# A fused attention and routed-layer kernel: the queue order and buffers of the weight pieces in its first stage

## The chip, the cores and the metric

The kernel runs on one core of one Trainium2 chip. The metric is the device time of one execution in microseconds (us). TensorE (PE) multiplies matrices, VectorE (DVE), ScalarE (ACT) and GpSimd (POOL) work element by element, and SyncE (SP) issues most transfers (DMA) between the device memory and the memory on the chip. Every engine has its own stream of instructions and works it off in order; semaphores tie the streams together.

## The reference, cut to what matters

```python
scale = 1.0 / np.sqrt(64)
p_packed = sm_attn(p, k, v)              # 32 packed queries per head over 576 keys; 8 batches, 8 heads
attn = sm_attn(q, p_packed, p_packed)    # 576 queries over the 32 packed rows
x = attn.transpose(0, 2, 1, 3).reshape(4608, 512)
h = x @ w_in                             # w_in 512 x 2048
x = (h - np.tanh(h)) @ w_out             # w_out 2048 x 512
logits = x @ w_gate                      # then: one of 8 experts for each token,
out = gate * eom * (relu(x @ w1[e]) @ w2[e])
```

q, k, v and p arrive as 32-bit floats. The weights w_in and w_out arrive as 64-bit floats, and the kernel narrows them to 32 bits itself, in pieces of 128 rows by 512 columns.

## The kernel before, in words

The program has three parts. **The first stage** computes the packed attention of p over k and v. It is cut into 16 units (`UNITS`), each for four heads of a batch, and its loop runs `u` from 0 to 17, so that the parts of one unit overlap those of its neighbours. In pass `u`, TensorE does the scores of unit `u` (`score`), the transposes of k for unit `u + 1` (`k_up`, three groups), and the product with v for unit `u - 2` (`pack`). VectorE takes the maximum (`expo`) and the transpose of the exponentials (`e_up`); ScalarE copies the transposed k, takes the exponential (`expo_b`) and scales the result of `pack`. The tiles are `kt` and `vt` (k and v as loaded), `kT`, `sc` (scores), `e_sb`, `eT`, `po` and `pp`. Beside that run `jobs`: the second attention of the first half batch, in steps `att_q`, `make_z`, `att_s`, `att_f`, `att_x`, `att_n`, `att_t`, `att_l`, and the product `fuse` of the packed rows with w_in.

In the same stage the weights are narrowed. `plan` lists 32 pieces, first 16 of w_in and then 16 of w_out. A piece is loaded into a staging tile `st` of 4 KB a partition (`load_w_in`, `load_w_out`), ScalarE takes the absolute value of its high words (L105), GpSimd bounds it from below (L106), and VectorE puts the words together in three steps (L111, L112, L114). Of a w_out piece, ScalarE and VectorE then make a high and a low part (`part_out`, L150 and L151). `NA` pieces are converted in the first stage, spread over the passes; `load_ahead(done)` issues loads until `NST` pieces more than those done are under way, and `NST` staging buffers turn in a circle.

**The second stage** works on halves of batches. Each half has 16 steps `f`: `up` (six matmuls), `up_b`, `down` (twelve matmuls), with 288 columns each; `drain` follows. Its first half also converts the pieces that the first stage left over, in steps 0 onwards, and does the second attention of the next half in steps 4 to 11. **The third part** routes tokens to experts. It isn't touched by the change.

What sets the order of work is the text of the program: each engine gets its instructions in the order in which the functions are called. All loads of k, v, p, q and the weights stand in SP's one queue, in that order, and a load whose buffer is still in use holds up all loads behind it.

```python
            want = (NA * u + LA - 2) // (LA - 1)
            for x, (_, conv, n) in enumerate(plan[done:want]):
                convert(done + x)
                if conv is conv_out:
                    late.append(n)
            done = want
            load_ahead(done)
            if u < 2:
                load_q(0, 0, [2 * u, 2 * u + 1])
```

Of the kernel before, what the change touches and what calls it, by code (L numbers as in the profile page):

```python
# [37 lines left out]
NST = 3  # L38
UNITS = 2 * NB
NA = 20  # L40
# [3 lines left out]
def attention_moe_kernel(ctx: ExitStack, tc: tile.TileContext, q, k, v, p, w_in, w_out, w_gate, w_og, w1, w2, out):  # L44
# [85 lines left out]
    wst, ist = {}, {}  # L130

    def load_w_out(f):
        rows = w_out[128 * f:128 * f + 128]
        if w_out.dtype == F32:
            wst[f] = cv.tile([128, DM], F32, name="wf")
            sp.dma_start(wst[f], rows)
        else:
            wst[f] = cv.tile([128, DM, 2], I32, name="st", bufs=NST)
            sp.dma_start(wst[f].rearrange("p n w -> p (n w)"), rows.bitcast(I32))
# [13 lines left out]
    def load_w_in(n):  # L153
        m, j = divmod(n, 4)
        rows, cols = slice(128 * j, 128 * j + 128), slice(512 * m, 512 * m + 512)
        if w_in.dtype == F32:
            sp.dma_start(w_in_sb[:, j, cols], w_in[rows, cols])
        else:
            ist[n] = cv.tile([128, 512, 2], I32, name="st", bufs=NST)
            sp.dma_start(ist[n].rearrange("p n w -> p (n w)"), w_in[rows, cols].bitcast(I32))  # L160
# [151 lines left out]
    def load_ahead(done):  # L312
        while ahead[0] < min(len(plan), done + NST):
            fn, _, n = plan[ahead[0]]
            fn(n)
            ahead[0] += 1
# [4 lines left out]
    with ExitStack() as pa:  # L321
# [3 lines left out]
        kp = pa.enter_context(tc.tile_pool(name="kp", bufs=3))  # L325
# [49 lines left out]
        load_ahead(1 - NST)  # L375
        load_k(1)
        load_ahead(2 - NST)
# [3 lines left out]
        load_ahead(0)  # L381
# [45 lines left out]
        for a in range(4):  # L427
            r = slice(32 * a, 32 * a + 32)
            pool.tensor_copy(fold[r], ident[r, r].rearrange("p (o c) -> p o c", o=1).to_broadcast([32, 4, 32]))
        jobs = {3: [lambda: att_q(0, 0)], 4: [lambda: make_z(0), lambda: att_s(0, 0)], 5: [lambda: att_f(0, 0), lambda: att_x(0, 0)],  # L430
                6: [lambda: att_n(0, 0), lambda: att_t(0, 0), lambda: fuse(0, 0)], 7: [lambda: att_l(0, 0), lambda: fuse_h(0, 0), lambda: fuse_l(0, 0)]}
        late, done = [], 0
        LA = UNITS + 2
        for u in range(LA):
# [8 lines left out]
            if u + 1 < UNITS:  # L443
                k_up(u + 1, 2)
            if 1 < u < UNITS + 2:
                pack(u - 2)
            if u + 1 < UNITS and (u + 1) % 4 == 0:
                make_p((u + 1) // 4)
            if u < UNITS:
                expo_b(u)  # L450
            for fn in jobs.get(u, ()):
                fn()
            if u + 3 < UNITS:
                load_k(u + 3)
            if 0 < u < UNITS:
                load_v(u)
            if u in (1, 5):
                load_p(2 + u // 4)
            if u % 4 == 2 and u < UNITS - 4:
                dup_p(u // 4 + 1)  # L460
            if u == 4:
                load_gates()
            if u == 7:
                vec.tensor_copy(wgt[:, :, 0:2 * NE], wgr)
# [9 lines left out]
            load_ahead(done)  # L474
            if u < 2:
                load_q(0, 0, [2 * u, 2 * u + 1])
# [4 lines left out]
    with ExitStack() as pb:  # L481
# [193 lines left out]
        for i, (b, hf) in enumerate(halves):  # L675
# [12 lines left out]
            if i == 0:  # L688
# [6 lines left out]
                for f in range(NF):  # L695
                    for x in part:
                        at(0, f, part_out, x)
                    part = []
                    take = plan[done:done + (2 if len(plan) - done > NF - 3 - f else 1)]
                    for x, (_, conv, m) in enumerate(take):  # L700
                        at(0, f, convert, done + x)
                        if conv is conv_out:
                            part.append(m)
                            assert f + 1 < m
                        else:
                            assert f < (0, 0, 4, 8)[m // 4]
                    done += len(take)
                    at(0, f, load_ahead, done)
# [469 lines left out]
```

## Time and profile before

| what | value |
|---|---|
| median of 3 runs | 1346.26 us (1340.08 to 1346.48) |
| the profiled execution, its own time | 1350.53 us |
| its span, first to last instruction | 1348.6 us |
| mean granted TensorE clock | 0.975 of full speed |
| busy: PE, DVE, ACT, POOL | 1264.3, 811.3, 515.1, 319.1 us |

The profile is that of one execution. Its times count from the span's start. A row of the timeline gives start, length, engine, source line, operation and operands, and in square brackets how long the engine stood idle before it and what ended the wait; "issue" there means that nothing which the profile shows was waited for. The granted clock is 1.00 at 2.4 GHz and 0.50 at 1.2 GHz. Loads of k and v are 576 KB each, those of weight pieces 512 KB. Engines that are not the bottleneck may idle at no cost, so the busy times are to be read by stage: the second stage begins at 122.71 us, with the first `up` matmul on TensorE.

### The profile page before, as it was taken

The page shows a single profiled execution, that of the slowest core. Times are in us where ns is not written, and L with a number is a line of the kernel's source. Part 1 is how long each engine was busy: PE and PEld are TensorE (multiplying, and loading weights), DVE is VectorE, ACT ScalarE, POOL GpSimd, SP SyncE. Part 2 cuts the span into 40 slices and gives each one's busy share as a digit, 9 for nine tenths or more (in the row PEclk, how much of TensorE's full clock was granted, in tenths as well). Part 3 has the DMA queues.
Part 4 walks back from the last instruction along what each step waited for, and adds up shares of the span by engine and source line. Part 5 has one row for each costly group of instructions (what it writes and reads, how often), then busy time and mean ns, then how long its engine had stood idle before and what let it go on. Part 6 is the DMA issues. An engine that isn't in the chain of part 4 may idle for free. (4 is left out here: it accounts for less than half of the span.)

```text
span 1348.6 us, 28576 instructions
## 1 busy us (share of the span) xinstructions
PE 1264.3 (94%) x10464; PEld 1084.6 (80%) x10464; DVE 811.3 (60%) x1823; ACT 515.1 (38%) x1109; POOL 319.1 (24%) x383
## 2 busy tenths in 40 slices
PE   6768779999999999999999999979999999999987
PEld 4556668998988989989899799757888788778765
DVE  4757887777777767777767867552333433433651
ACT  4344444344344343443434445332223322422431
POOL 4323311001010010100100111124443544354531
PEclk8789889999999999999999999989999999999999
DMA  8874524014122140142203134521113311412331
GB/s 254 292 255 150 143 49 25 13 36 36 32 25 17 36 36 7 35 32 36 30 8 54 19 50 116 130 76 40 48 39 106 108 48 39 161 50 94 125 143 42
DMA packets 135757, 102.42 MB, mean 76 GB/s; under 512 B 96784, under 2 KB 115220, under 8 KB 134964
## 3 DMA queue, kind: packets, MB, share of 16 engines
q1 hardware_dynamic: 125908, 80.33, 25.4%
q0 software_dynamic: 9696, 20.14, 5.1%
q8 instruction: 85, 1.39, 0.5%
q14 instruction: 68, 0.56, 0.2%
HBM read 215.60 MB, written 19.57 MB: 174 GB/s over the span
## 5 line engine op out<-in xcount | busy, mean ns | idle before, releaser
L616 POOL DMA_INDIRECT tab<-tok,ix x48 | 55.0, 1146 | 614.0 <-DVE ix L613 566.0
L883 DVE TENSOR_TENSOR hl<-pt,hh 128x512 fp32r<-128x512 f32 x76 | 52.3, 689 | 191.2 <-ACT hh L882 180.6
L522 ACT ACTIVATE gh<-gg 128x288 fp32r<-128x288 f32 x256 | 112.7, 440 | 142.0 <-PE acc L537 95.7
L523 DVE TENSOR_TENSOR gl<-gg,gh 128x288 fp32r<-128x288 f32 x256 | 115.4, 451 | 81.6 <-ACT gh L522 76.1
L509 PE MATMUL ph<-a_hi,wf_hi 128*128 128x288 f32 x512 | 160.1, 313 | 3.0 <-ACT wf_hi L240 3.0
L536 PE MATMUL acc<-gl,wo_bt 128*128 128x288 f32 x512 | 155.4, 304 | 4.4 <-DVE gl L523 4.0
L511 PE MATMUL ph<-a_hi,wf_lo 128*128 128x288 f32 x512 | 152.0, 297 | 5.5 <-DVE wf_lo L244 5.5
L515 DVE TENSOR_TENSOR gg<-ph,th 128x288 f32<-128x288 f32 x256 | 115.9, 453 | 68.5 <-ACT th L513 66.9
L535 PE MATMUL acc<-gh,wo_a 128*128 128x288 f32 x512 | 151.5, 296 | 2.0 <-ACT gh L522 2.0
L536 PE MATMUL acc<-gl,wo_a 128*128 128x288 f32 x512 | 151.9, 297 | 1.3 <-DVE gl L523 1.3
L535 PE MATMUL acc<-gh,wo_bt 128*128 128x288 f32 x512 | 152.2, 297 | 0.6 <-ACT gh L522 0.6
L510 PE MATMUL ph<-a_lo,wf_hi 128*128 128x288 f32 x512 | 151.8, 297 | 0.8 <-issue 0.8
L537 PE MATMUL acc<-gh,wo_bt 128*128 128x288 f32 x512 | 152.0, 297 | 0.0
L537 PE MATMUL acc<-gh,wo_a 128*128 128x288 f32 x512 | 151.7, 296 | 0.0
L827 POOL DMA_INDIRECT xg<-x2d,iq x132 | 135.1, 1023 | 61.1 <-issue 52.9
L513 ACT ACTIVATE th<-ph 128x288 f32<-128x288 f32 x256 | 104.1, 407 | 113.7 <-PE ph L511 92.8
L871 ACT ACTIVATE h<-ph 128x512 f32<-128x512 f32 x76 | 45.0, 597 | 249.8 <-PE ph L870 199.3
L509 PEld LDWEIGHTS ph<-a_hi,wf_hi 128*128 128x128 f32 x512 | 96.6, 189 | 45.2 <-issue 39.5
L869 PE MATMUL ph<-w1l,xh 128*128 128x512 f32 x304 | 121.3, 399 | 6.8 <-DVEq L1004 5.9
L892 PE MATMUL py<-w2h,hh 128*128 128x512 f32 x304 | 126.1, 415 | 0.2
L893 PE MATMUL py<-w2l,hh 128*128 128x512 f32 x304 | 120.3, 396 | 1.7 <-DVE w2l L788 1.7
L894 PE MATMUL py<-w2h,hl 128*128 128x512 f32 x304 | 120.6, 397 | 0.7 <-DVE hl L883 0.7
(220 smaller groups left out, 2715.4 us busy)
## 6 DMA issues: line engine op xcount, KB each, us to landing
raw<-in_moe_w_dram SPq DMA_DIRECT2D x37, 2048.0 KB
sraw<-in_moe_w_dram SPq DMA_DIRECT2D x37, 1024.0 KB
x2s<-in_moe_w_dram SPq DMA_DIRECT2D x37, 1024.0 KB
kt<-in_k_dram SPq DMA_DIRECT2D x16, 576.0 KB
vt<-in_v_dram SPq DMA_DIRECT2D x16, 576.0 KB
x2d<-x2s SPq DMA_DIRECT2D x64, 144.0 KB
qt<-in_q_dram SPq DMA_DIRECT2D x240, 36.0 KB
st<-in_moe_w_in_dram SPq DMA_DIRECT2D x16, 512.0 KB
```

The source lines that it names most:

```text
L509: pe.matmul(ph, lhsT=wf_hi[n][:, g, c], rhs=ah[:, g], start=g == 0, stop=False)
L510: pe.matmul(ph, lhsT=wf_hi[n][:, g, c], rhs=al[:, g], start=False, stop=False)
L511: pe.matmul(ph, lhsT=wf_lo[n][:, g, c], rhs=ah[:, g], start=False, stop=g == 1)
L515: vec.tensor_tensor(gg, ph, th, op=ALU.subtract)
L535: pe.matmul(acc[j], lhsT=hi[:, j], rhs=gh, start=f == 0, stop=False)
L536: pe.matmul(acc[j], lhsT=hi[:, j], rhs=gl, start=False, stop=False)
L537: pe.matmul(acc[j], lhsT=lo[:, j], rhs=gh, start=False, stop=f == NF - 1)
L827: pool.indirect_dma_start(xg[:, g], None, src, bass.IndirectOffsetOnAxis(ap=iq[:, g:g + 1].bitcast(U32), axis=0))
L869: pe.matmul(ph, lhsT=xh[:, c], rhs=w1l[:, c, r], start=False, stop=False)
L892: pe.matmul(py, lhsT=hh[:, c], rhs=w2h[:, c], start=c == 0, stop=False)
L893: pe.matmul(py, lhsT=hh[:, c], rhs=w2l[:, c], start=False, stop=False)
L894: pe.matmul(py, lhsT=hl[:, c], rhs=w2h[:, c], start=False, stop=c == 7)
```

## The change

The change does six things. It raises `NA` from 20 to 24. It gives the staging tiles of the first 24 pieces two buffers more (`NX`, a pool `cx`, so five in all) and k four buffers instead of three. It moves `load_ahead` from the end of a pass, behind that pass's conversions, to a place ahead of them and behind the loads of k and v, with the count of pieces done up to the pass before. It loads q one part in each of passes 2 to 5, instead of two parts in each of passes 0 and 1, and moves `jobs` from passes 3 to 7 to passes 6 to 10. It loads k of unit 3 and v of unit 1 before the loop. And it puts the exponential `expo_b` ahead of `pack` and `make_p` in a pass. In the second stage `load_ahead` moves ahead of the step's conversion in the same way.

```diff
+NX = 2
-NA = 20
+NA = 24
...
+    extra = {}
+
+    def stage(i):
+        pl = extra["pool"] if i < NA and i % (NST + NX) >= NST else cv
+        return pl.tile([128, 512, 2], I32, name="st", bufs=NX if pl is not cv else NST)
+
-            wst[f] = cv.tile([128, DM, 2], I32, name="st", bufs=NST)
+            wst[f] = stage(i)
...
-            ist[n] = cv.tile([128, 512, 2], I32, name="st", bufs=NST)
+            ist[n] = stage(i)
...
     def load_ahead(done):
-        while ahead[0] < min(len(plan), done + NST):
+        while ahead[0] < len(plan) and ahead[0] < done + NST + (NX if ahead[0] < NA else 0):
             fn, _, n = plan[ahead[0]]
-            fn(n)
+            fn(n, ahead[0])
             ahead[0] += 1
...
-        kp = pa.enter_context(tc.tile_pool(name="kp", bufs=3))
+        kp = pa.enter_context(tc.tile_pool(name="kp", bufs=4))
+        extra["pool"] = pa.enter_context(tc.tile_pool(name="cx", bufs=1))
...
         load_k(0)
         load_p(0)
-        load_ahead(1 - NST)
+        load_ahead(1 - NST - NX)
         load_k(1)
-        load_ahead(2 - NST)
+        load_ahead(2 - NST - NX)
         load_v(0)
         load_k(2)
         load_p(1)
-        load_ahead(0)
+        load_ahead(3 - NST - NX)
+        load_k(3)
+        load_v(1)
...
-        jobs = {3: [lambda: att_q(0, 0)], 4: [lambda: make_z(0), lambda: att_s(0, 0)], 5: [lambda: att_f(0, 0), lambda: att_x(0, 0)],
-                6: [lambda: att_n(0, 0), lambda: att_t(0, 0), lambda: fuse(0, 0)], 7: [lambda: att_l(0, 0), lambda: fuse_h(0, 0), lambda: fuse_l(0, 0)]}
+        jobs = {6: [lambda: att_q(0, 0)], 7: [lambda: make_z(0), lambda: att_s(0, 0)], 8: [lambda: att_f(0, 0), lambda: att_x(0, 0)],
+                9: [lambda: att_n(0, 0), lambda: att_t(0, 0), lambda: fuse(0, 0)], 10: [lambda: att_l(0, 0), lambda: fuse_h(0, 0), lambda: fuse_l(0, 0)]}
...
+            if u < UNITS:
+                expo_b(u)
             if 1 < u < UNITS + 2:
                 pack(u - 2)
             if u + 1 < UNITS and (u + 1) % 4 == 0:
                 make_p((u + 1) // 4)
-            if u < UNITS:
-                expo_b(u)
-            for fn in jobs.get(u, ()):
-                fn()
-            if u + 3 < UNITS:
+            if 0 < u and u + 3 < UNITS:
                 load_k(u + 3)
-            if 0 < u < UNITS:
+            if 1 < u < UNITS:
                 load_v(u)
+            load_ahead(done)
             if u in (1, 5):
                 load_p(2 + u // 4)
+            if 1 < u < 6:
+                load_q(0, 0, [u - 2])
...
+            for fn in jobs.get(u, ()):
+                fn()
...
             done = want
-            load_ahead(done)
-            if u < 2:
-                load_q(0, 0, [2 * u, 2 * u + 1])
...
+                    if f:
+                        at(0, f, load_ahead, done)
                     take = plan[done:done + (2 if len(plan) - done > NF - 3 - f else 1)]
...
-                    at(0, f, load_ahead, done)
```

SP's queue, from its ninth load on, before (`kt`, `vt` are k and v, `st` a weight piece, `scr` of q or p):

```order
L160 DMA st<-in_moe_w_in_dram 128x1024
L257 DMA kt<-in_k_dram 128x1152
L187 DMA scr<-in_q_dram 32x9x32 x8
L257 DMA kt<-in_k_dram 128x1152
L262 DMA vt<-in_v_dram 128x1152
L371 DMA scr<-in_p_dram 128x4x64
L160 DMA st<-in_moe_w_in_dram 128x1024 x2
L187 DMA scr<-in_q_dram 32x9x32 x8
L257 DMA kt<-in_k_dram 128x1152
L262 DMA vt<-in_v_dram 128x1152
```

And with the change, from the same load on:

```order
L166 DMA st<-in_moe_w_in_dram 128x1024
L263 DMA kt<-in_k_dram 128x1152
L268 DMA vt<-in_v_dram 128x1152
L166 DMA st<-in_moe_w_in_dram 128x1024 x2
L263 DMA kt<-in_k_dram 128x1152
L378 DMA scr<-in_p_dram 128x4x64
L263 DMA kt<-in_k_dram 128x1152
L268 DMA vt<-in_v_dram 128x1152
L166 DMA st<-in_moe_w_in_dram 128x1024 x2
L193 DMA scr<-in_q_dram 32x9x32 x4
```

The sixth load of k, the next to last `kt` row in both lists, stood behind sixteen transfers of q and behind two weight pieces that wait for a conversion; it now stands behind weight pieces with free buffers, and ahead of all q.

ScalarE in the first stage, passes 1 to 3 before (`cvt<-st` is the first step of a conversion):

```order
L291 ACTIVATE e_sb,rs<-sc,mx 128x576
L105 ACTIVATE cvt<-st 128x512 x3
L271 ACTIVATE kT<-pk 128x384 x3
L306 ACTIVATE pp<-po,rs 128x64
L291 ACTIVATE e_sb,rs<-sc,mx 128x576
L105 ACTIVATE cvt<-st 128x512
L271 ACTIVATE kT<-pk 128x384 x3
L306 ACTIVATE pp<-po,rs 128x64
L387 ACTIVATE scr<-pk 128x512
L291 ACTIVATE e_sb,rs<-sc,mx 128x576
L105 ACTIVATE cvt<-st 128x512
```

And with the change:

```order
L297 ACTIVATE e_sb,rs<-sc,mx 128x576
L106 ACTIVATE cvt<-st 128x512 x3
L277 ACTIVATE kT<-pk 128x384 x3
L297 ACTIVATE e_sb,rs<-sc,mx 128x576
L312 ACTIVATE pp<-po,rs 128x64
L106 ACTIVATE cvt<-st 128x512
L277 ACTIVATE kT<-pk 128x384 x3
L297 ACTIVATE e_sb,rs<-sc,mx 128x576
L312 ACTIVATE pp<-po,rs 128x64
L396 ACTIVATE scr<-pk 128x512
L106 ACTIVATE cvt<-st 128x512 x2
```

The exponential `e_sb` went ahead of `pp`, which waits for the end of `pack`; and pass 3 has two conversions where it had one.

VectorE in the second stage's first half, from the maximum of step 8 to step 10, with the change (`gl` and `gg` are the step's own work, `cvt` conversions, of which none is left here):

```order
L214 TENSOR_REDUCE amx<-sT 128x18
L215 TENSOR_TENSOR sT<-sT,amx 128x576
L157 TENSOR_TENSOR wo_bt<-cvt,wo_bt 128x512
L532 TENSOR_TENSOR gl<-gg,gh 128x288
L524 TENSOR_TENSOR gg<-ph,th 128x288
L250 TENSOR_TENSOR wf_lo_2340<-px,wf_hi_2339 128x512 x2
L222 TENSOR_REDUCE asm<-ex 128x18
L223 TENSOR_SCALAR asm<-asm 128x18
L224 RECIPROCAL asm<-asm 128x18
L225 TENSOR_TENSOR ex<-ex,asm 128x576
L532 TENSOR_TENSOR gl<-gg,gh 128x288
L524 TENSOR_TENSOR gg<-ph,th 128x288
```

Before, three conversion instructions and one `wo_bt` stood at the end of each of the steps 8 to 11; with the change the last conversion is in step 7 and its `wo_bt` in step 8.

## Rows read from the trace of the kernel before

**Rows 1.** Windows by stretch: length, busy us (instructions) by engine, clock, DMA share, GB/s
```profile
0.00:23.20 23.20, 16.16 (x260) 12.72 (x261) 6.45 (x11) 10.50 (x22) 11.36 (x35) 0.85 0.85 277
77.20:98.20 21.00, 12.43 (x343) 9.17 (x344) 9.44 (x22) 6.78 (x17) 3.69 (x4) 0.80 0.89 325
80.00:85.00 5.00, 3.92 (x42) 2.67 (x45) 2.59 (x7) 1.47 (x3) 1.46 (x2) 0.50 1.01 390
167.90:189.70 21.80, 13.69 (x73) 12.54 (x73) 18.85 (x35) 9.04 (x19) 5.05 (x4) 0.83 0.35 76
199.80:240.00 40.20, 40.20 (x335) 35.53 (x334) 29.10 (x72) 16.91 (x41) 4.19 (x6) 1.00 0.37 26
```

**Rows 2.** Timeline, PE, first stage: start, length, idle before and its releaser
```profile
34.47 2.15 PE L270 MATMUL pk<-ident,kt 128*128 128x128 f32 x9 [3.43 <-DMA kt<-in_k_dram]
...
48.40 1.18 PE L303 MATMUL po<-vt,eT 32*32 32x64 f32 x55 [2.79 <-issue]
...
81.08 1.18 PE L280 MATMUL sc<-kT,scr 64*32 64x288 f32 x5 [3.17 <-issue]
...
95.44 1.22 PE L303 MATMUL po<-vt,eT 32*32 32x64 f32 x73 [3.59 <-issue]
...
104.62 0.96 PE L280 MATMUL sc<-kT,scr 64*32 64x288 f32 x16
105.51 1.20 PE L270 MATMUL pk<-ident,kt 128*128 128x128 f32 x9
...
109.09 0.68 PE L303 MATMUL po<-vt,eT 32*32 32x64 f32 x33 [0.69 <-issue]
109.70 0.72 PE L280 MATMUL sc<-kT,scr 64*32 64x288 f32 x16
...
114.92 0.72 PE L280 MATMUL sc<-kT,scr 64*32 64x288 f32 x16 [0.22 <-ACT kT L271]
...
119.96 0.52 PE L303 MATMUL po<-vt,eT 32*32 32x64 f32 x20 [1.29 <-DMA vt<-in_v_dram]
```

**Rows 3.** DMA queues from 0 to 122.7 us: packets, MB, share of 16 engines
```profile
q1 hardware_dynamic: 14461, 30.47, 72.7%
q8 instruction: 20, 0.33, 1.0%
```

**Rows 4.** Waits, 20 to 123 us: who waited for whom, us, times, longest
```profile
PE po L303 <- issue: 9.0, 6, 3.6
...
PE sc L280 <- issue: 5.8, 2, 3.2
PE pk L270 <- DMA kt<-in_k_dram: 3.4, 1, 3.4
...
PE sc L280 <- ACT e_sb L291: 1.4, 1, 1.4
```

**Rows 5.** Timeline, SP: the loads around k of unit 5
```profile
24.27 5.97 SPq L187 DMA_DIRECT2D scr<-in_q_dram  x8
30.34 0.40 SPq L257 DMA_DIRECT2D kt<-in_k_dram  x1
```

**Rows 6.** Costliest groups, DVE, 0 to 123 us: busy, mean ns
```profile
L112 DVE SCALAR_TENSOR_TENSOR cvt<-st,cvt 128x512 int32<-128x512 int32 x18 | 12.8, 712 | 0.6
L114 DVE SCALAR_TENSOR_TENSOR w_in_sb<-st,cvt 128x512 int32<-128x512 int32 x16 | 11.4, 710 | 0.5
L111 DVE TENSOR_SCALAR cvt<-cvt 128x512 int32<-128x512 int32 x18 | 8.9, 495 | 11.6 <-POOL cvt L106 11.6
L151 DVE TENSOR_TENSOR wo_a<-cvt,wo_a 128x512 fp32r<-128x512 f32 x1 | 0.7, 692 | 1.7 <-ACT wo_a L150 1.7
```

**Rows 7.** Timeline, DVE: a pass with two conversions
```profile
107.97 0.82 DVE L111 TENSOR_SCALAR cvt<-cvt 128x512 int32<-128x512 int32 x1 [4.82 <-POOL cvt L106]
```

**Rows 8.** Timeline, DVE, second stage, first half: steps 8 and 12 begin
```profile
167.95 0.45 DVE L523 TENSOR_TENSOR gl<-gg,gh 128x288 fp32r<-128x288 f32 x1
...
189.72 0.45 DVE L523 TENSOR_TENSOR gl<-gg,gh 128x288 fp32r<-128x288 f32 x1
```

More of the change, by code (lines that the diff above doesn't have):

```diff
@@ L130, in attention_moe_kernel, with load_w_out @@
     wst, ist = {}, {}
-    def load_w_out(f):
+    extra = {}
+    def stage(i):
+        pl = extra["pool"] if i < NA and i % (NST + NX) >= NST else cv
+        return pl.tile([128, 512, 2], I32, name="st", bufs=NX if pl is not cv else NST)
+    def load_w_out(f, i):
         rows = w_out[128 * f:128 * f + 128]
@@ L151, in part_out, with load_w_in @@
         vec.tensor_tensor(lo, sv, hi, op=ALU.subtract)
-    def load_w_in(n):
+    def load_w_in(n, i):
         m, j = divmod(n, 4)
```

## The prediction

> **What bounds the kernel now.** I read the busy time by stretch first. From 199.8 us on TensorE is busy in all 40.20 of 40.20 us [rows 1], and the rest of the second stage looks the same, so whatever the front of the program gains or loses reaches the end one for one. The change acts ahead of that, in two stretches with different limits.
>
> In the first stage (0 to 122.7 us) no engine is full. Between 77.2 and 98.2 us TensorE is busy 12.43 of 21.00 us, VectorE 9.44, ScalarE 6.78; up to 23.2 us it is 16.16 of 23.20, VectorE 6.45 [rows 1]. The transfers are the busiest resource, with a share of 0.89 in the one stretch and 72.7% over the whole stage [rows 1, 3], but they too have pauses. What the reader is to see in TensorE's timeline are the pauses between passes: 3.43 us for k of unit 5, and stops of 2.79 and 3.59 us in the middle of a row of identical `pack` matmuls, put down to "issue" [rows 2]. Nothing in the program can be waited for there. The stage fetches 20 blocks of instructions by DMA [rows 3]; the reading that fits is that TensorE stands until the next block has come, and that a block comes late while the DMA engines are full. The same kind of stop is 0.69 us at 109 us, where they are nearly empty [rows 2]. Such stops sum to 9.0 + 5.8 = 14.8 us [rows 4], and a long one is followed by the lower of the two levels of TensorE's clock: behind the stop of 3.17 us that ended at 81.08 us [rows 2], the granted clock is 0.50, or 1.2 GHz, from 80 to 85 us [rows 1]. That is why it is 0.80 to 0.85 over these stretches.
>
> In the first half of the second stage, VectorE sets the pace in the steps 8 to 11: 18.85 of 21.80 us busy, TensorE 13.69 [rows 1], and these four steps take 189.72 - 167.95 = 21.77 us [rows 8]. A later half takes about 40.2 / 16 = 2.5 us a step with TensorE full [rows 1].
>
> **The change part by part. Four pieces leave the second stage.** A conversion is three VectorE instructions, 0.495 + 0.712 + 0.710 = 1.92 us by their means, and the split of a w_out piece is another 0.692 [rows 6]; 2.6 us each, 10.4 us for four. They sit in steps 8 to 11 of a stretch that VectorE fills, so they are on the path. From the other side: at 2.5 us a step, with the two extras there (the fused weights and the sums of the attention) still costing 1 to 1.5 us each, the four steps would take about 12 us, so 21.8 - 12 = 9.8. I take **-10**. The bounds are -5 (VectorE's 2.95 us idle in the four steps stays, and the chain through ScalarE's exponential takes 2 us of the rest) and -12 (all steps at 2.5 us: 21.8 - 10).
>
> **Four pieces enter the first stage.** By the same rows that is 7.7 us of conversion and, for the three of them split before the end, 2.1 us: between 0, when they fill VectorE's idle time (9.44 of 21.00 us busy), and +9.8, all on the path. They come mostly as passes with two conversions, seven instead of three. There the second one waits for ScalarE and GpSimd: 4.82 us in the pass at 105 to 110 us [rows 7]. Yet TensorE's pass there took 109.70 - 104.62 = 5.08 us, and the next, with one conversion, 5.22 [rows 2], so what reaches TensorE is about 1 us (the product behind it waited for ScalarE's scaling). Four more such passes: **+4**. This is nearer to the lower bound since that pass is the nearest row.
>
> **The queue.** k of unit 5 was issued at 30.34 us, behind eight q transfers that took 5.97 us to issue [rows 5]; in the new order it stands ahead of all q, and its buffer, of four, is free early. The wait of 3.43 us goes: **-3.4**. v for the last product stood behind weight pieces waiting for conversions; its 1.29 us [rows 2] goes: **-1.3**. After the first 20 us these two are TensorE's only waits for k or v [rows 2, 4]. The weights themselves come two pieces earlier, but VectorE did not wait for them in the middle of the stage, so deeper staging gives nothing by itself. The order of the first eight loads is the same, hence also the start.
>
> **The exponential ahead of pack.** One wait of TensorE for it is shown, 1.4 us [rows 4]: **-1.4**. It also releases the scores one `pack` earlier, which I cost at nothing, since two score buffers cover it; if they don't, it is a further gain.
>
> **The later jobs** move the same VectorE work from passes 3 to 7 to passes 6 to 10; cost 0, covered by VectorE's idle time in 77.2 to 98.2 us [rows 1]. If that cover goes, passes 8 and 10, which have both a job and two conversions, last some 2 us longer each. SP's transfers are as many as before, four weight pieces excepted: 4 x 512 KB at the 325 GB/s of a full stretch [rows 1] are 6.5 us of transfers, in a stage where the engines of DMA stand idle for 27% of 122.7 us, or 33 us [rows 3]. A weight load that waits for a conversion still holds up the k and v behind it on SP, but those are now the next pass's, needed two passes later.
>
> **The instruction stops** I leave as they are. They depend on how full the DMA engines are when a block is asked for; the added 6.5 us raise the share from 0.73 to about 0.78 if the stage lasts as long. Bounds: all 14.8 us gone, or twice as many. Here the row shows stops up to 3.59 us [rows 2]. The Trainium skill (Runtime: NRT & Kernel Launch, "Instruction fetch mechanics") says that instructions stream in blocks of 16 KiB while the current one runs, the cost "mostly hidden". By that rule the stops have another cause, one in the queue that the change may clear, and the sum would be about -11 in the first stage; the trace speaks against it, as the stops lie inside one group of matmuls.
>
> **The sum.** First stage: +4 - 3.4 - 1.3 - 1.4 = -2.1, say -2. Second stage: -10. Together -12 on the profiled execution's own time of 1350.5 (span 1348.6 and 1.9 around it): 1338.5. That execution stands 4.3 above the median of the runs shown; from the median 1346.3 the forecast is **1334 us**. Its own range is 1326 to 1341.
>
> **The rivals.** *The stage runs freely.* If transfers that no longer queue behind conversions also end most of the stops and the low clock after them, the first stage goes to what its loops need. From 23.2 us on come thirteen passes at 5.2 us [rows 2], six of them 1 us longer for the second conversion, some 8 us more for what of the jobs VectorE can't hide (an estimate), and 6.5 us for the last products, which is what they take now: 23.2 + 67.6 + 6 + 8 + 6.5 = 111 us, so -11, and with -10 in the second stage -21: 1325 us. For it: passes at 104 to 119 us did run so. Against: they ran so beside nearly empty DMA engines.
>
> *The stops multiply.* With five staging buffers and four of k, SP has a load in the engines almost always, and each of the 20 fetches, TensorE's and the others', can meet one. Eight such stops are in the stage now [rows 4]. A long one costs some 2.7 us more than one beside empty engines, and 1.7 us more by the low clock behind it (half of a stretch at half speed: `k_up` took 2.15 us behind the wait at 34 us and 1.20 at 105 us [rows 2], and a `pack` loses about as much): some 4.4 each. Three more outweigh the gain of 12; five more give +22, so about 1356 us, slower. For it: the stops did come with full engines. Against: the same bytes per pass, and a fetch is passed on a queue of its own, so that the length of SP's queue need not matter.
>
> *The pieces are paid for where they go.* VectorE's path in the first stage carries all 9.8 us, seven double passes in a row with the jobs, while the queue's gain of 6.1 and the 10 of the second stage stand against it, less 3 us that the next piece arrives late in steps 2 and 3, since it now queues behind sixteen transfers of q: -3 to -6, about 1342 us, within the noise.
>
> *It doesn't do what it says*: the extra buffers are used only if SP isn't stopped elsewhere. Then the queue terms go and -10 + 4 = -6 is left, 1340 us; I put that with the case before.
>
> **How the numbers follow.** Chances: forecast 0.46, free stage 0.23, paid for 0.21, stops multiply 0.10. A difference of 0.5% (6.7 us) is about what a measurement of this kernel can tell from none. Faster by more: most of the forecast (0.40), the free stage (0.23), a little of the third case (0.05): 0.68. Slower by more: the stops (0.09): 0.09. The rest, 0.23, is within. The range runs from 1317, the bounds of both stages together with some of the stops gone (-12 and -17), to 1346, no change; what is left out is most of the stops case and the ends of the others.
>
> **What would show it.** Right: the second stage's first `up` at 118 to 123 us; no wait for `kt` after 20 us; SP's weight loads waiting little for VectorE; steps 8 to 11 of the first half in about 12 us. The forecast is wrong if the second stage starts before 115 or after 128 us, or if steps 8 to 11 still take over 16 us. Fewer or more stops put down to "issue", and the clock behind them, tell the first two rivals apart.

## The result, and the profile after

| | before | changed | ratio, 95% interval |
|---|---|---|---|
| median of 5 runs each | 1343.05 us (1340.08 to 1346.48) | 1334.43 us (1333.02 to 1337.38) | 0.9919 [0.9893, 0.9945] |
| the profiled execution, and its span | 1350.53, 1348.6 | 1334.43, 1332.7 | |
| mean granted TensorE clock | 0.975 | 0.982 | |

The ratios and intervals, here and below, are those on record. A ratio is an estimate of its own and not the quotient of the two medians, which is 0.9936 here; the two differ by up to 0.0024 (3 us).

The change makes the kernel faster by 8.6 us at the medians. The profiled executions differ by 15.9 us in span, but not all of that is the change's: behind the first half's drain the span is 1150.1 us before and 1146.4 after, and the other traces of the same two kernels have 1142.0 and 1136.6 there. So the traces are compared up to that drain, which starts at 198.46 us before and at 186.33 us after.

Windows of the kernel after. The columns are those of [rows 1]; the stretches are the same 21 us of the first stage, the end of it (from the scores of the last unit to the first step of the second stage), the steps 8 to 11, and a later half:

```profile
77.20:98.20 21.00, 16.23 (x506) 13.07 (x505) 17.40 (x35) 11.47 (x27) 6.74 (x5) 0.80 0.73 262
109.20:137.68 28.48, 19.36 (x516) 16.42 (x514) 24.77 (x49) 13.92 (x31) 10.60 (x7) 0.88 0.44 129
165.37:177.72 12.35, 9.49 (x57) 8.80 (x57) 9.64 (x20) 5.38 (x12) 0.00 (x0) 0.86 0.00 1
187.90:228.10 40.20, 40.20 (x335) 35.53 (x334) 28.99 (x73) 16.86 (x40) 4.20 (x6) 1.00 0.34 30
```

The third row is the largest gain: steps 8 to 11 take 12.35 us where they took 21.77 [rows 8], and VectorE is busy 9.64 us in them instead of 18.85 [rows 1]. The fourth is the same as before: TensorE is full there. The second is where the four pieces are paid for: VectorE is busy 24.77 of 28.48 us.

TensorE's timeline of the kernel after, first stage; columns as in [rows 2]:

```profile
23.43 1.59 PE L276 MATMUL pk<-ident,kt 128*128 128x128 f32 x9 [2.54 <-DMA kt<-in_k_dram]
...
42.36 0.75 PE L309 MATMUL po<-vt,eT 32*32 32x64 f32 x38 [3.15 <-issue]
...
48.97 2.36 PE L309 MATMUL po<-vt,eT 32*32 32x64 f32 x80 [3.05 <-issue]
...
75.68 1.54 PE L286 MATMUL sc<-kT,scr 64*32 64x288 f32 x16 [2.71 <-ACT e_sb L297]
...
92.33 1.22 PE L286 MATMUL sc<-kT,scr 64*32 64x288 f32 x16 [3.68 <-ACT scr L396]
...
109.20 0.72 PE L286 MATMUL sc<-kT,scr 64*32 64x288 f32 x16
113.19 3.62 PE L309 MATMUL po<-vt,eT 32*32 32x64 f32 x144 [3.27 <-ACT pp L312]
118.90 0.40 PE L518 MATMUL ph<-a_hi,wf_hi 128*128 128x288 f32 x1 [2.09 <-ACT e_sb L297]
```

The wait for k of unit 5 [rows 2] is gone; one of 2.54 us for unit 4 stands eleven us earlier. The stops inside a group are still there. The last scores start at 109.20 us, 5.7 us earlier than before (114.92 [rows 2]), yet the first `up` comes at 118.90, only 3.8 us earlier.

The transfers' queues of the kernel after from 0 to 122 us, columns as in [rows 3]:

```profile
q1 hardware_dynamic: 15040, 32.58, 77.6%
q8 instruction: 20, 0.33, 1.1%
```

The share is 77.6% where it was 72.7% [rows 3]. The waits of the kernel after from 20 to 123 us, as in [rows 4]:

```profile
PE po L309 <- issue: 8.8, 4, 3.1
DVE wo_a L157 <- ACT wo_a L156: 5.9, 3, 4.0
...
PE sc L286 <- ACT scr L396: 4.4, 2, 3.7
...
PE sc L286 <- ACT e_sb L297: 2.7, 1, 2.7
PE pk L276 <- DMA kt<-in_k_dram: 2.5, 1, 2.5
...
PE sc L286 <- issue: 2.3, 2, 1.3
```

New here are the waits of TensorE for ScalarE's copies (4.4 us) and of VectorE for ScalarE's half of a split (5.9 us, the longest 4.0).

VectorE's timeline of the kernel after, the end of the first stage and then three marks of the second: the gated products with which the steps 1, 8 and 12 begin, and the drain:

```profile
117.83 0.77 DVE L301 STREAM_TRANSPOSE eT<-e_sb 128x576 f32<-128x576 f32 x1
...
119.80 0.69 DVE L157 TENSOR_TENSOR wo_a<-cvt,wo_a 128x512 fp32r<-128x512 f32 x1 [0.96 <-ACT wo_a L156]
120.41 0.42 DVE L112 TENSOR_SCALAR cvt<-cvt 128x512 int32<-128x512 int32 x1
...
122.48 0.83 DVE L112 TENSOR_SCALAR cvt<-cvt 128x512 int32<-128x512 int32 x1
...
124.69 0.77 DVE L301 STREAM_TRANSPOSE eT<-e_sb 128x576 f32<-128x576 f32 x1
...
137.68 0.45 DVE L532 TENSOR_TENSOR gl<-gg,gh 128x288 fp32r<-128x288 f32 x1
...
165.37 0.45 DVE L532 TENSOR_TENSOR gl<-gg,gh 128x288 fp32r<-128x288 f32 x1
...
177.72 0.46 DVE L532 TENSOR_TENSOR gl<-gg,gh 128x288 fp32r<-128x288 f32 x1 [0.22 <-ACT gh L531]
...
186.33 1.65 DVE L554 STREAM_TRANSPOSE x2s<-acc 128x288 f32<-128x288 f32 x4
```

Between the last two transposes of the exponentials, on which the last products with v wait, stand a split and two conversions: 6.86 us from the one to the other. Before, it was one conversion and a split, and 5.37 us. The same transposes, the mark of step 1 and the drain in VectorE's timeline of the kernel before:

```profile
118.12 0.77 DVE L295 STREAM_TRANSPOSE eT<-e_sb 128x576 f32<-128x576 f32 x1
...
123.49 0.77 DVE L295 STREAM_TRANSPOSE eT<-e_sb 128x576 f32<-128x576 f32 x1
...
136.05 0.44 DVE L523 TENSOR_TENSOR gl<-gg,gh 128x288 fp32r<-128x288 f32 x1
...
198.46 1.65 DVE L545 STREAM_TRANSPOSE x2s<-acc 128x288 f32<-128x288 f32 x4
```

The mark of step 1 comes at 137.68 us, 1.6 later than before (136.05).

These marks cut the front of the program into five lengths, in us, each the difference of two starts on TensorE's or VectorE's timeline. The table has them for the kernels that follow, but for the last one, one trace each; the ratio is the one on record, to the kernel before on the same chip.

| kernel | to the last scores | end of stage 1 | steps 1-7 | 8-11 | 12 to drain | drain at | ratio |
|---|---|---|---|---|---|---|---|
| before | 114.9 | 21.1 | 31.9 | 21.8 | 8.7 | 198.5 | 1 |
| before, again | 111.7 | 24.4 | 31.4 | 21.8 | 8.8 | 198.0 | 0.9986 |
| changed | 109.2 | 28.5 | 27.7 | 12.4 | 8.6 | 186.3 | 0.9919 |
| changed, again | 113.2 | 30.1 | 28.2 | 12.0 | 8.2 | 191.7 | 0.9901 |
| changed, 20 pieces | 113.8 | 26.3 | 28.4 | 21.8 | 8.8 | 199.0 | 0.9966 |
| changed, three staging buffers | 116.2 | 28.5 | 31.5 | 12.3 | 8.6 | 197.1 | 0.9944 |
| changed, old place of the weight loads | 116.7 | 28.9 | 28.1 | 12.7 | 8.6 | 195.0 | 0.9977 |
| changed, old places of q and jobs | 113.4 | 28.6 | 27.8 | 12.0 | 8.2 | 190.0 | 0.9980 |
| changed, exponential behind `pack` | 112.5 | 30.3 | 28.2 | 12.0 | 8.2 | 191.2 | 0.9907 |
| changed, splits ahead of `pack` | 109.4 | 28.5 | 28.3 | 12.0 | 8.1 | 186.5 | 0.9902 |
| the same, first steps two pieces ahead | 109.5 | 28.9 | 28.3 | 12.0 | 8.2 | 186.9 | 0.9890 |
| before, 24 pieces | 118.2 | 30.3 | 30.9 | 12.1 | 8.2 | 199.6 | 0.9994 |
| before, 24 pieces, five buffers | 115.3 | 30.5 | 31.8 | 12.6 | 8.6 | 198.8 | 1.0024 |

The column of steps 8 to 11 has the pieces in it and repeats to 0.3 us. The end of the stage has them too, 28.5 us or more with 24 pieces and 26.3 or less with 20, but it differs by up to 3.3 us between two traces of one kernel, and the first column by 3 to 4. So a single row's first two columns, and with them its drain, say less than the ratio.

### The profile page after: what moved, and what is told of

It reads as the page before. It is cut to its first block, busy times and chain, and to the rows that moved or that the text cites. A ratio compares the mean times of both kernels' runs of the same rounds, so it can differ in the third digit from the quotient of the medians.

```text
span 1332.7 us, 28571 instructions
## 1 busy us (share of the span) xinstructions
PE 1259.2 (94%) x10464; PEld 1081.7 (81%) x10464; DVE 814.1 (61%) x1823; ACT 516.7 (39%) x1109; POOL 320.6 (24%) x383
## 5 line engine op out<-in xcount | busy, mean ns | idle before, releaser
L524 DVE TENSOR_TENSOR gg<-ph,th 128x288 f32<-128x288 f32 x256 | 116.2, 454 | 68.4 <-ACT th L522 67.0
```

Of the source, the lines that this page charges most:

```text
L524: vec.tensor_tensor(gg, ph, th, op=ALU.subtract)
```

## The experiments

**The kernels again.** The kernel before, unchanged, for a second trace:

> The kernel before, unchanged, for a second trace of it. Theory: the length of its first stage is not one number; which instruction stops fall where differs between executions by several us, as it did for the changed kernel, while the second stage repeats. So the first step's gated product, at 136.05 us in the first trace, should come 3 us or more earlier or later, with other stops in TensorE's timeline, and the steps 8 to 11 should again take 21.8 us (within 0.3). The part behind the drain of the second stage, which the change does not touch, should take the same as in the other kernels of its chip (1136 to 1151 us). Rival: the first stage repeats within 1 us, and then the difference of 1.6 us between the first traces of the two kernels is the change's own.

Measured: 0.9986 [0.9960, 1.0011]. The mark of step 1 is at 136.06 us, so the rival held on that number, and steps 8 to 11 take 21.78. But the parts of it moved: the last scores came 3.2 us earlier, the end of the stage was as much longer, and TensorE's stops were others (20.2 us in twelve up to 8 us behind the first `up`, where the first trace has 17.0 in ten; all sums of stops below are counted like this). The changed kernel again:

> The changed kernel itself once more, beside the runs that follow, since the first stage of single executions differs by some us. Both theories: ratio to the kernel before 0.990 to 0.995. If the stops differ from execution to execution, its first stage ends within 7 us of the first profile's, with other stops.

Measured: 1327.06 against 1337.11 us on that chip, 0.9901 [0.9867, 0.9935]. Its first stage was 5.6 us longer in this trace (mark of step 1 at 143.26), with 14.7 us of stops where the first trace has 11.1. Steps 8 to 11 took 12.04.

**The number of pieces alone**, both ways. First 20 pieces in the changed kernel:

```diff
-NA = 24      # in the changed kernel
+NA = 20
```

> The changed kernel with 20 pieces in the first stage instead of 24: the queue order, the buffers, the later jobs and the earlier exponential alone. Theory of the forecast (the pieces moved out of VectorE's full steps carry the gain): steps 8 to 11 of the second stage's first half last 21 to 22 us again, not 12.4, the first stage ends a few us earlier than with 24 pieces; in all 2 to 6 us below the kernel before, ratio 0.995 to 0.999. Rival (the queue carries the gain, the number of pieces does not matter): the time is that of the changed kernel, ratio about 0.992.

Measured: 1332.79 against 1337.24 us, 0.9966 [0.9952, 0.9981]. VectorE's timeline of this kernel, marks of the steps 8 and 12:

```profile
168.50 0.45 DVE L532 TENSOR_TENSOR gl<-gg,gh 128x288 fp32r<-128x288 f32 x1
...
190.28 0.45 DVE L532 TENSOR_TENSOR gl<-gg,gh 128x288 fp32r<-128x288 f32 x1
```

The 21.8 us are back. Of what is left of the gain, 4.5 us, the steps 1 to 7 have 3.2 (28.4 us in place of 31.9 and 31.4). The first stage was expected to end earlier than with 24 pieces, and in this trace it did not: its mark of step 1, at 140.07, lies between the changed kernel's 137.68 and 143.26. But this execution stands 5.7 us above the median of its kernel and has the most stops of all, 22.9 us, one of them at the end of the stage in TensorE's timeline:

```profile
124.10 3.63 PE L309 MATMUL po<-vt,eT 32*32 32x64 f32 x127 [4.87 <-issue]
```

Then 24 pieces in the kernel before:

```diff
-NA = 20      # in the kernel before
+NA = 24
```

> The kernel before with 24 pieces in the first stage instead of 20 and nothing else. Theory of the forecast: steps 8 to 11 fall from 21.8 to about 12.4 us, the first stage grows by 4 to 6 us since its queue still blocks; in all 4 to 9 us below the kernel before, ratio 0.993 to 0.997. Rival (the queue carries the gain): what the steps lose comes back in the first stage, ratio 1.000 or above.

Measured: 1335.49, 0.9994 [0.9978, 1.0011]. VectorE's timeline, marks of the steps 1, 8 and 12:

```profile
148.52 0.45 DVE L523 TENSOR_TENSOR gl<-gg,gh 128x288 fp32r<-128x288 f32 x1
...
179.42 0.45 DVE L523 TENSOR_TENSOR gl<-gg,gh 128x288 fp32r<-128x288 f32 x1
...
191.47 0.45 DVE L523 TENSOR_TENSOR gl<-gg,gh 128x288 fp32r<-128x288 f32 x1
```

Two lines of its waits, up to 135 us and from 135 to 200 us:

```profile
ACT cvt L105 <- DMA st<-in_moe_w_in_dram: 8.3, 2, 6.2
...
ACT cvt L105 <- DMA st<-in_moe_w_out_dram: 7.0, 3, 4.5
```

The second stage gives the forecast 10 us (12.05 in place of 21.77), and in this trace the first stage takes 12.5 back, not the 4 to 6 expected: its mark is at 148.52. With three buffers and the old order, ScalarE, which begins a conversion, waits for the pieces.

**Three staging buffers** in the changed kernel:

```diff
-        pl = extra["pool"] if i < NA and i % (NST + NX) >= NST else cv
+        pl = cv
...
-        while ahead[0] < len(plan) and ahead[0] < done + NST + (NX if ahead[0] < NA else 0):
+        while ahead[0] < len(plan) and ahead[0] < done + NST:
...
```

> The changed kernel with three staging buffers for all pieces instead of five; the order of loads, 24 pieces and four buffers of k as in the changed kernel. Theory of the forecast (deeper staging gives nothing by itself, since VectorE did not wait for pieces): within 2 us of the changed kernel, ratio 0.990 to 0.994. Rival (the buffers are what lets the first stage keep up): conversions wait for their pieces, ScalarE shows waits for st, and the first stage ends 5 us or more later, ratio 0.996 or above.

Measured: 1330.31, 0.9944 [0.9926, 0.9962]. ScalarE's waits for pieces, up to 135 us and then from 135 to 200 us:

```profile
ACT cvt L106 <- DMA st<-in_moe_w_in_dram: 14.2, 4, 4.5
...
ACT cvt L106 <- DMA st<-in_moe_w_out_dram: 6.4, 2, 4.9
```

In the changed kernel these waits are 0 and 0.3 us. So the two buffers seem worth some 3 to 6 us here (0.9944 against 0.9901 and 0.9919; the intervals overlap), though the prediction found no wait of VectorE for pieces. The ratio lies between the two expectations; the waits of ScalarE are those of the rival.

**The place of the weight loads** undone for the first stage, with all buffers, the places of q and the loads ahead of the loop kept:

```diff
-            load_ahead(done)          # behind load_k and load_v
...
+            load_ahead(done)          # at the end of the pass
```

> The changed kernel with the weight loads of a pass at its end again, behind that pass's conversions, with the newer count of pieces done; five buffers, 24 pieces and the rest as changed. Theory after the first runs (what carries 24 pieces is the staging depth): ratio to the kernel before 0.988 to 0.994, like the changed kernel, no wait of ScalarE for st over 2 us in the first stage. Rival (the place behind k and v carries it): k and v are held up by weight loads, waits for kt or vt come back, ratio 0.995 or above.

Measured: 1344.58 against 1346.51 us, 0.9977 [0.9955, 0.9998]. TensorE's stops in this kernel, 20 to 123 us:

```profile
PE po L309 <- issue: 15.8, 6, 3.5
...
PE sc L286 <- issue: 4.6, 2, 3.3
```

Most of the gain is gone, and there is no wait for pieces: it is not staging depth alone that carries the change. Nor did the waits of the rival come: TensorE's waits for k and v, up to 135 us, come to 3.9 + 0.9 us, where those for k are 4.2 and 3.3 in the two traces of the changed kernel. The larger difference in this trace is in the stops, 20.4 us against 11.1 and 14.7 in the changed kernel. Whether the old order brings such stops or this execution had them by chance, one trace can't say, so how the old place costs time stays open; the ratio rests on twelve runs.

**The places of q and the jobs** undone:

```diff
-        jobs = {6: [...], 7: [...], 8: [...], 9: [...], 10: [...]}
+        jobs = {3: [...], 4: [...], 5: [...], 6: [...], 7: [...]}
...
-            if 1 < u < 6:
-                load_q(0, 0, [u - 2])
...
+            if u < 2:
+                load_q(0, 0, [2 * u, 2 * u + 1])
```

> The changed kernel with the jobs in passes 3 to 7 and q loaded in passes 0 and 1 again, as before the change. Theory of the forecast (moving the jobs costs and gives nothing by itself; q ahead of k costs 3 us): 0 to 5 us above the changed kernel, a wait for kt or q of 2 to 4 us in the first 40 us. Rival (jobs beside fewer transfers give more): over 5 us above, ratio 0.995 or above.

Measured: 1342.01, 0.9980 [0.9965, 0.9995]. TensorE's waits for k up to 135 us:

```profile
PE pk L276 <- DMA kt<-in_k_dram: 8.2, 3, 4.3
```

In the two traces of the changed kernel these waits are 4.2 and 3.3 us, so with sixteen transfers of q in the first two passes k comes 4 to 5 us later in all. By the ratio this part, for which the prediction charged or credited nothing but the k of unit 5, is worth as much as any other. The trace shows no such loss: its drain, at 190.0, lies between the changed kernel's 186.3 and 191.7, though this execution is 3.0 us below the median of its kernel. And q and the jobs were put back together, so which of them counts is not shown.

**Buffers and pieces without the order**, in the kernel before:

```diff
+NX = 2
-NA = 20
+NA = 24
...
+        pl = extra["pool"] if i < NA and i % (NST + NX) >= NST else cv
...
```

> The kernel before with 24 pieces and five staging buffers, and nothing else of the change: order of loads, three buffers of k, jobs and the exponential as before. Theory after the first runs (pieces and staging depth together are the change): ratio 0.989 to 0.994, ScalarE waits for st under 2 us in the first stage. Rival (the order behind k and v, the place of q, or k's fourth buffer is needed as well): ratio 0.996 or above, with waits for st, kt or vt of 5 us or more.

Measured: 1349.86 against 1346.51 us, 1.0024 [1.0007, 1.0042]. Two of its waits, for k up to 135 us and for pieces from 135 to 200 us:

```profile
PE pk L277 <- DMA kt<-in_k_dram: 5.5, 3, 2.4
...
ACT cvt L106 <- DMA st<-in_moe_w_out_dram: 5.2, 1, 5.2
```

The pieces and the buffers are in this kernel, the second stage's 9 us are there (12.6), and the time is no better than before: the first stage takes all of it, with its mark of step 1 at 145.72, 9.7 us later. ScalarE waits for no piece in the first stage, and the waits for k are no longer than in the kernel before (7.1 and 6.6 us in its two traces); what grew is the end of the stage, 30.5 us.

**Two small edits.** The exponential put back behind `pack`:

```diff
-            if u < UNITS:
-                expo_b(u)
             if 1 < u < UNITS + 2:
                 pack(u - 2)
...
+            if u < UNITS:
+                expo_b(u)
```

> The changed kernel with the exponential behind pack and make_p again, as before the change; all else as changed. Theory of the forecast (this edit gives 1.4 us): 0 to 3 us above the changed kernel. Rival (it is this edit that lets the first stage carry four more pieces, since pack and pp no longer hold the exponential): 5 us or more above the changed kernel, the first stage ending that much later.

Measured: 1327.15, 0.9907 [0.9875, 0.9940], against 0.9901 with it ahead: nothing that can be told. And the splits of w_out pieces, for which VectorE waits 5.9 us, put ahead of `pack`:

```diff
+            for n in late:
+                part_out(n)
+            late = []
             if 1 < u < UNITS + 2:
                 pack(u - 2)
...
-            for n in late:
-                part_out(n)
-            late = []
```

> The changed kernel with the split of w_out pieces ahead of pack in a pass, so that ScalarE's part of it no longer queues behind pp and VectorE's part no longer waits for it. Theory (the four pieces cost the first stage some us by such waits in its last passes): VectorE's wait for wo_a in the first stage falls from 5.9 us to under 2, and the time falls by 2 to 5 us below the changed kernel. Rival (the last passes are held by VectorE's work itself or by stops): within 1.5 us of the changed kernel.

Measured: 1326.14, 0.9902 [0.9869, 0.9935]. Up to 135 us the wait falls to 3.6 us from 6.7 and 7.0 in the traces of the changed kernel, and the time stays the same. On top of it, the first steps of a conversion two pieces ahead instead of one:

```diff
+        if i + 2 < 16:
+            clamp_next(i + 2)
```

> As the run with the split ahead of pack, and ScalarE and GpSimd start on a w_in piece two pieces ahead instead of one. Theory (in passes with two conversions VectorE waits for GpSimd, 6.6 us in the changed kernel): that wait falls under 2 us, and the time falls by 1 to 4 us more. Rival (the wait is covered): within 1 us of the run with the split ahead of pack.

Measured: 1324.24, 0.9890 [0.9850, 0.9929]; the lowest median on that chip, but not told apart from the changed kernel's 0.9901 [0.9867, 0.9935]. Nor did the wait go: VectorE waits 7.2 us for GpSimd from 20 to 123 us, where the changed kernel has 6.6 and 14.9 and the run with the splits ahead 10.5.

**Most loads of k and v left out**, two fifths of the bytes, to see what the stops hang on:

```diff
     def load_k(u):
+        if u > 3:
+            k_t[u] = k_t[u % 4]
+            return
```

and the same for v from unit 3 on.

> The changed kernel without the loads of k from unit 4 on and of v from unit 3 on; the units use the first four and three tiles again, so the outputs are not the reference's. It takes 15 MB of the first stage's 33 MB of transfers away and no instruction of TensorE. Theory of the stops (instruction blocks come late while the DMA engines are full): no stop put down to issue is over 1.5 us in the first stage, their sum falls from 11 us to under 5, the granted clock is at least 0.95 there, and the stage ends 6 to 12 us earlier. Rival (the stops have another cause): stops of about 3 us remain, and the end moves by less than 3 us.

The third part has other tokens to route here, so only the first stage is compared, in one execution. TensorE's two longest stops in its timeline up to 118 us:

```profile
36.52 0.70 PE L292 MATMUL sc<-kT,scr 64*32 64x288 f32 x11 [2.32 <-issue]
...
97.85 0.53 PE L315 MATMUL po<-vt,eT 32*32 32x64 f32 x23 [1.05 <-issue]
```

The transfer queues of the same kernel from 0 to 122 us:

```profile
q1 hardware_dynamic: 11728, 18.88, 49.2%
q8 instruction: 21, 0.34, 1.2%
```

As many blocks of instructions come (21), but the stops sum to 4.6 us in five, where the two traces of the changed kernel have 11.1 and 14.7. The mark of step 1 is at 131.53 us, 6.2 and 11.7 us earlier than in those, the granted clock of the first 123 us is 0.90 (0.88 in those), not the 0.95 expected. So most of the stops go with the transfers. They are not all of what the first stage loses: one of 2.32 us is left, and its end still takes 29.2 us, as VectorE's conversions are the same.

What TensorE waits for in a stop can be read from the traces too, which have the time of each transfer of the queue q8. In the four traces of the two kernels 35 of the 36 stops end 1.0 to 1.7 us after a block of instructions has landed. The stop of 3.59 us in the kernel before [rows 2] lasts from 91.85 to 95.44 us, and its block was under way from 93.08 to 94.04. In the stops of over 2 us the transfer, some 1 us like the others, begins between 0.5 us ahead of the stop's start and 1.4 behind it. So TensorE stands until its next block has come, as the prediction read it. What delays the transfer's start is not in the records.

## Why the prediction was right, and which of its steps were not

Forecast 1334, measured 1334.43. That they agree to half a microsecond is luck: the forecast took -12 us from a median of 1346.3 us, of three runs; that of the five is 1343.05, and the medians moved by -8.6 [ratio 0.9919] and, on another chip, by -10.0 [0.9901]. The direction and the largest term were right. In the rest of the sum two errors partly cancel: the first stage was forecast shorter and came out longer, and a gain in the second stage was not forecast. From the means of two traces each (the first four rows of the table): the first stage up to step 1 is 4.4 us longer (forecast: 2 shorter), steps 1 to 7 are 3.7 shorter (forecast: nothing), steps 8 to 11 are 9.6 shorter (forecast: 10), the rest 0.4 shorter. That is -9.2 in all.

**Four pieces leave the second stage: right.** -9.6 for -10, steps of 12.35 and 12.04 us for "about 12". All kernels with 24 pieces have 12.0 to 12.7 us there, the three with 20 have 21.8. VectorE did set that pace.

**Four pieces enter the first stage: read from the wrong place; the size is open.** The prediction took 1 us for each of four passes, +4, from a pass (104.62 to 109.70) behind which others follow, bounds 0 and +9.8. The cost came behind the last scores. The window of that stretch in the first trace of the kernel before, to set beside the 28.48 us above:

```profile
114.90:136.05 21.15, 16.72 (x514) 13.63 (x514) 16.79 (x37) 11.03 (x27) 9.11 (x6) 1.00 0.54 169
```

And in the second trace of the same kernel:

```profile
111.68:136.06 24.38, 19.21 (x517) 16.02 (x514) 16.08 (x34) 11.55 (x27) 8.55 (x5) 0.86 0.42 141
```

VectorE's work there goes from 16.79 and 16.08 to 24.77 us (25.12 in the second trace of the changed kernel), and the stretch from 21.1 and 24.4 to 28.5 and 30.1: +6.5 by the means. Until then VectorE has idle time to give; at the end the last transposes stand behind the conversions in its stream, and TensorE has little else to do. That +6.5 is not the price of the pieces alone. With 20 pieces and all the rest of the change the stretch is 26.3, of which 6.1 are two stops, and VectorE is busy 14.65 in it. From that kernel to the changed one the time falls by 6 to 9 us by the ratios (0.9966 to 0.9919 and 0.9901), by 4 to 6 by the quotients of medians, while steps 8 to 11 give 9.6: the first stage keeps 1 to 5.5 us of it, with the forecast +4 inside. In the old order it keeps nearly all (0.9994). So the terms that failed in the first stage are rather the gains of 6.1 us set against the pieces: with 20 pieces, where they should show alone, 4.5 us of gain are measured, 3.2 of them in the steps 1 to 7.

**The queue: -4.7 forecast, partly right.** The wait of 3.43 us for k of unit 5, the last `kt` row in both lists of SP's queue, and that of 1.29 us for v [rows 2] are gone (the latter is 0.25 us in the second trace of the kernel before). A new one for k of unit 4 takes 2.54 us; SP issued that load at 11.80 us, while the engines of DMA were full (share 0.93 up to 23.2 us). All waits for k, up to 135 us, fall from 7.1 and 6.6 us to 4.2 and 3.3. "No wait for `kt` after 20 us" was wrong in the first trace of the changed kernel and right in the second. "Weight loads waiting little for VectorE" was wrong: SP's waits for VectorE at them sum to 48.3 us in 13 up to 123 us (71.9 in 17 before). What changed is what stands behind them. To the last scores the stage is 2.1 us shorter by the means of two traces, less than those two traces differ by (109.2 and 113.2).

**"Deeper staging gives nothing by itself": wrong.** The reason given, that VectorE did not wait for pieces, looked at the wrong engine. ScalarE starts a conversion and does wait. Its waits for pieces from 123 to 200 us, before and then after:

```profile
ACT cvt L105 <- DMA st<-in_moe_w_out_dram: 8.4, 4, 4.4
...
ACT cvt L106 <- DMA st<-in_moe_w_out_dram: 0.3, 1, 0.3
```

That is where the gain of 3.7 us in steps 1 to 7 comes from: in the kernels of the table in which these waits are 5 us or more, the steps 1 to 7 take 30.9 us or more, and in the others, with waits of 2.1 us or less, 28.4 or less. It takes both the five buffers and a load issued ahead of the step's conversion: with the load's place alone, steps 1 to 7 take 31.5 us, with the buffers alone 31.8. In the first stage three buffers with 24 pieces bring 14.2 us of such waits.

**The later jobs and q, "cost 0": wrong by the ratio.** With both put back, 2.7 us of the gain are left by the ratio (0.9980), 4.5 by the medians; the trace doesn't show the loss. The prediction saw what the jobs do to VectorE, and of q only the one load behind which k of unit 5 stood.

**The exponential, -1.4: not seen.** Without it the ratio is 0.9907, and TensorE's wait for it did not go: 2.7 and 2.3 us in the two traces with the edit, 1.4 in both before it.

**The stops: neither fewer for sure nor multiplied.** 17.0 and 20.2 us in the traces before, 11.1 and 14.7 after, with a share of transfers of 77.6% against 72.7% [rows 3]. The rival that they multiply fell. The rival of the free stage fell as well: 118.9 and 123.2 us to the first `up`, not 111. (Its passes at 104 to 119 us ran beside a share of 0.60; "nearly empty" holds from 106 to 110 us, 0.05.) That of the pieces paid where they go was right on its place, VectorE's path in the first stage, and wrong on the total, since it left out the steps 1 to 7. The Trainium skill (Runtime: NRT & Kernel Launch, "Instruction fetch mechanics") calls the cost of streaming instructions "mostly hidden"; the traces here disagree: the stops end as blocks land, and they sum to 11 to 20 us in a stage of some 120 us with a share of transfers of 73 to 78%.

**"That is why" the clock is 0.80 to 0.85: only in part.** Up to 23.2 us there is no stop in any of the four traces, and the clock is 0.85 in one trace of each kernel and 1.00 in the other. Waits for other engines are followed by the lower level as well: behind the one of 3.27 us for `pp` the clock is 0.58 and a `pack` of 144 matmuls takes 3.62 us, where one at 112.48 us in the kernel before takes 2.21 at 1.00.

**The parts are not a sum.** Undone one by one, the pieces give back 6 to 9 us, the buffers 3 to 6, the place of the weight loads 8 to 10, the places of q and the jobs 8 to 11 (ratios against 0.9901 and 0.9919, of 1340 us; by the quotients of medians each is 1 to 5 us less; the last two on a chip on which the changed kernel itself was not run). Together that is about two to three times the gain: the second stage's 10 us come with 24 pieces every time, and reach the end only if the first stage can take the pieces, for which, by the ratios, it needs the others as well.

28 pieces in the first stage were not tried: the second halves of the parts of w_out get their place only in the second stage. Nor were k's fourth buffer, the two loads ahead of the loop, q and the jobs each undone alone. Open are two things: how much of what the old place of the loads costs comes from the stops, and why step 1's mark in two traces of the changed kernel lies 5.6 us apart (3.7 more of stops, and a clock of 0.85 instead of 1.00 up to 23.2 us, go with it) while that of the kernel before repeats.

## What to carry to other kernels

When work moves from a stretch that an engine fills to one where no engine is full, look at the end of the second one: here the price showed in its last passes, behind which nothing hides it. To see whether loads come late, look at the engine that touches the loaded tile first, and not at the one that does most of the work on it. A change whose parts clear the way for each other should be costed as a whole, and one part alone may show nothing or a loss, as 24 pieces alone (0.9994) and with buffers (1.0024) did.

## What the runs showed of the hardware

The stops of TensorE that are put down to "issue" end 1.0 to 1.7 us after a block of instructions has landed (35 of 36). They come with busy DMA engines and not with the number of such blocks: 21 blocks and 4.6 us of stops at a share of 49.2% for the data queue, 20 blocks and 11.1 us at 77.6%. Their places and sum differ between executions of one kernel (11.1 and 14.7, 17.0 and 20.2 us), while the steps 8 to 11 of the second stage repeat to 0.3 us. And the part behind the drain, which is the same in both kernels, took 1136.6 to 1150.1 us in the four traces of them. Traces from one chip agree there (1133.6 to 1136.6 us in four kernels, 1147.2 to 1150.7 in three on another), so the difference is mostly the chip's, and times of this kernel are to be compared on one chip only.
